# Attention before an FFN: chunks of 120 keys and paired heads, or chunks of 56 keys and four heads at a time

## The chip, the core and the metric

The kernel runs on one core of a Trainium2 chip. TensorE multiplies, VectorE (DVE) and ScalarE (ACT) do elementwise work, GpSimd (POOL) issues DMAs that convert fp32 to fp16 on the way, and SyncE (SP) and ScalarE issue DMAs that don't. The metric is the device time of one execution in microseconds; lower is better. A profiled execution has a span (first to last instruction) and a time of its own that is a little longer.

## The reference, cut to what matters

Batch 4, 8 heads, 768 positions, head size 64, 8 global keys, a local window of 96, and an FFN from 512 to 1536 and back over 3072 tokens:

```python
    scores = scale * np.matmul(q, k.transpose(0, 1, 3, 2))
    rel = pos[:, None] - pos[None, :]
    is_global = pos[None, :] < int(n_global)
    is_local = (rel >= 0) & (rel < int(n_local))
    keep = is_global | is_local
    dist = np.where(is_global & ~is_local, float(n_local), np.abs(rel).astype(np.float32))
    slopes = 2.0 ** (-8.0 * (np.arange(H, dtype=np.float32) + 1) / H)
    scores = scores - slopes[:, None, None] * dist[None, :, :]
    scores = np.where(keep, scores, -1000000000.0)
    a = np.exp(scores - np.max(scores, axis=-1, keepdims=True))
    a = a / (np.sum(a, axis=-1, keepdims=True) + 1e-09)
    attn_out = np.matmul(a, v)
    x = attn_out.transpose(0, 2, 1, 3).reshape(B * S, H * D)
    g = x @ w_gate
    silu = g * (1.0 / (1.0 + np.exp(-g)))
    out = (silu * (x @ w_val)) @ w_out
```

## The kernel before, in words

The whole program is one list of steps, the string `ORDER`. Each step is a name and its arguments (`g.0.3` is the gate product of token block 0, hidden block 3), and the loop at the end calls the function that belongs to the name. Every engine works through its own instructions in the order in which the list issues them, so the list sets the order on all engines and on the DMA queues.

**Attention.** The keys stand in 7 chunks of 120. A chunk is 128 columns of `kTs`: the 8 global keys and 120 local ones. The queries that a chunk can see are a window of 216, cut at the ends. `scores` (step `c`) puts a chunk's keys on the 128 rows of PSUM, for the two heads of a pair at once: head 0 on the upper 64 rows of TensorE, head 1 on the lower (64x128 tiles). The distances enter in one of two ways. For some units of batch 0, `bias` (step `B`) adds slope times distance by a matmul with `slopeI` before the scores; for all others `mask` (step `m`) multiplies the exponentials by `masks`, the exponential of minus slope times distance. `exps` (step `x`) is the exponential on ScalarE, to fp16 tiles `at`. `weigh` (step `w`) sums `at` over the keys for four heads at a time on 128x32 tiles: what 0 with ones (the denominators, `den`), what 1 and 2 with the even and odd columns of the values (`num`). For most halves `take_num` (step `n`) copies `num` out of PSUM on ScalarE. `invert` and `spread` (steps `i`, `r`) transpose the denominators on VectorE, take reciprocals and spread them, and `scaled` (step `p`) multiplies into `xT`, the input of the FFN.

**FFN.** A token block is 384 tokens, half a batch, and there are 8. For each of 12 hidden blocks: gate product `g` and value product `v` (4 matmuls of 384 columns each), tanh on ScalarE (`t`), two operations on VectorE (`s`, `h`). The output product `o` has 36 matmuls of 512 columns per token block, in parts of three, and `e` copies and stores.

**Loads.** `ld_first` (`Lf`) loads half of the keys and queries of batch 0's first half as fp32 by SP and ScalarE, and `cast` converts them on VectorE or ScalarE. All else of q, k, v and the weights comes by GpSimd with conversion: `Lh`, `L4`, `Lr` for q and k, `Lv` for v, `Lw` and `Lo` for the weights. Batch 0 and half of batch 1 are transposed by TensorE (`T`, `U`) and copied out (`k`, `q`, `kw`, `qw`); the other half of batch 1 and batches 2 and 3 by DMA transposes on SP (`D`), after which `K` spreads the keys into chunks on VectorE. `fill` issues matmuls on ones, which compute nothing that is used.

**PSUM.** Two double tiles take the scores and `num`, four single ones all else. They are handed out in the order in which they come free.

Of the kernel before, what the change touches and what calls it, by code (L numbers as in the profile page):

```python
# [14 lines left out]
FAR = 60000.0  # L15
KC = 120
WIN = 216
BANK = 432


def _build_dist(S, NG, NL):


    row = np.arange(128)[:, None]
# [8 lines left out]
    d = np.concatenate([first, inner, inner[:, :168], inner[:, :48]], axis=1)  # L33
# [16 lines left out]
T.3.1.0 Lw.0.2.0 k.3.1.V T.3.1.1 g.0.6 w.0.0.1.0 c.0.2.2 Lw.0.2.1 Lw.1.1.1 t.0.6 i.0.0.1 s.0.6  # L50
r.0.0.1 Lw.1.2.0 c.0.2.3 g.0.7 Lr.1.1.7 q.3.1.A x.0.2.2 v.0.2 h.0.2 w.0.0.1.1 t.0.7 s.0.7 w.0.0.1.2
# [73 lines left out]
def kernel(  # L125
# [110 lines left out]
    def release(key):  # L236
        freed.append(busy.pop(key))
# [442 lines left out]
```

## Time and profile before

| | us |
|---|---|
| runs | 253.18, 252.24, 250.27; median 252.24 |
| the profiled execution | 250.97 |
| its span | 249.2 |

| engine | busy us | share of the span |
|---|---|---|
| TensorE matmul (PE) | 237.3 | 95% |
| VectorE (DVE) | 174.0 | 70% |
| ScalarE (ACT) | 119.4 | 48% |
| GpSimd (POOL) | 77.7 | 31% |

In the profile's lines, `L530` is line 530 of the kernel; `num<-at,vS` names what is written and read; `128*32` behind a matmul is its tile of TensorE (rows x columns), and `128x216` its moving operand. A group's row gives its count, its busy time and the mean ns of one, then the time that its engine stood idle just before such instructions and what ended it. A line of the chain that ended last gives start, length and what ran. Timelines put instructions of a kind together and show in brackets how long the engine had been idle and what released it. Matmuls overlap, so a busy TensorE is not one at its peak rate.

### The profile page before, as it was taken

Reading aid. Unit: us, or ns where it says so; the run is one execution under the profiler, and the core shown is the slowest. Engines: PE = TensorE matmul, PEld = TensorE weight load, DVE = VectorE, ACT = ScalarE, POOL = GpSimd, SP = SyncE. Lnnn points to the kernel's source line nnn. Section 1 sums busy time; section 2 is a strip of 40 time slices with the busy share of each in tenths; the row PEclk is TensorE's granted clock in tenths of the full one; section 3 lists DMA queues with packets and bytes.
Section 4 is the critical chain, followed back from the end, with each engine's and each line's share of the span. In section 5 each row is a group of like instructions: output and inputs, shape, how many; then the busy total and the mean of one; then the engine's idle time right before and its main releaser. Section 6 shows DMA issues by size and latency. Waiting matters only on the chain.

```text
span 249.2 us, 5795 instructions
## 1 busy us (share of the span) xinstructions
PE 237.3 (95%) x2368; PEld 134.1 (54%) x2368; DVE 174.0 (70%) x407; ACT 119.4 (48%) x216; POOL 77.7 (31%) x99
## 2 busy tenths in 40 slices
PE   7999999997899999999999999999999899899993
PEld 4565656654455545555555565565555654455552
DVE  6598899838878696848796588789675748566210
ACT  3677773863666423575264454456464233223310
POOL 8995665762898564650000000000000000000000
PEclk9999999999999999999999999999999999999999
DMA  8999999999999999999202214120110111010202
GB/s 182 166 198 190 205 198 195 175 134 151 202 157 121 138 131 153 171 168 104 74 3 74 86 35 116 25 76 0 45 42 0 45 45 42 1 42 3 84 21 107
DMA packets 88715, 25.56 MB, mean 103 GB/s; under 512 B 78536, under 2 KB 85744, under 8 KB 88688
## 3 DMA queue, kind: packets, MB, share of 16 engines
q0 software_dynamic: 67520, 13.81, 70.2%
q1 hardware_dynamic: 20480, 10.86, 21.4%
q10 hardware_dynamic: 688, 0.52, 0.7%
q8 instruction: 18, 0.29, 0.5%
q14 instruction: 9, 0.07, 0.1%
HBM read 28.58 MB, written 6.29 MB: 140 GB/s over the span
## 4 chain that ended last, share of the span: by engine, by line
PE 77%; DMA 11%; DVE 9%; issue 1%; ACT 1%; SPq 0%; DVEq 0%; ACTq 0%
PE vps L576 22%; PE ops L610 21%; PE gps L576 21%; DMA kN<-kst 7%; PE sc L471 4%; DMA qT<-qst 3%; PE num L530 3%; DVE xT L562 2%; PE den L530 2%; PE sc L458 2%; DVE at L498 2%; DVE hT L592 2%; PE trs L361 1%; DMA k<-in_k_dram 1%; PE ops L607 1%
## 5 line engine op out<-in xcount | busy, mean ns | idle before, releaser
L576 PE MATMUL gps<-xT,wg 128*128 128x384 f16 x384 | 73.9, 326 | 2.2 <-DVE xT L562 1.6
L582 ACT ACTIVATE th<-gps 128x384 f32<-128x384 f32 x96 | 46.5, 492 | 57.5 <-PE gps L576 55.4
L576 PE MATMUL vps<-xT,wv 128*128 128x384 f16 x384 | 72.7, 326 | 0.0
L592 DVE TENSOR_TENSOR hT<-vps,sl 128x384 f16<-128x384 f32 x96 | 51.8, 553 | 26.0 <-PE vps L576 24.5
L586 DVE SCALAR_TENSOR_TENSOR sl<-th,gps 128x384 f32<-128x384 f32 x96 | 52.1, 548 | 20.8 <-ACT th L582 19.7
L610 PE MATMUL ops<-wo,hT 128*128 128x512 f16 x276 | 66.7, 379 | 0.0
L576 PEld LDWEIGHTS <-wg 128*128 128x128 f16 x384 | 36.2, 98 | 29.4 <-issue 4.0
L576 PEld LDWEIGHTS <-wv 128*128 128x128 f16 x384 | 36.5, 98 | 26.8 <-issue 0.9
L481 ACT ACTIVATE at<-sc 128x864 f16<-128x864 f32 (+2 forms) x52 | 41.9, 835 | 14.1 <-PE sc L471 14.1
L610 PEld LDWEIGHTS <-hT 128*128 128x128 f16 x276 | 26.3, 98 | 27.9 <-issue 0.4
L624 ACT ACTIVATE osb<-ops 128x512 f32<-128x512 f32 x23 | 13.8, 598 | 35.2 <-PE ops L610 35.1
L259 POOL DMA_DIRECT2D vS<-in_v_dram x28 | 25.1, 900 | 10.4 <-DMA kst<-in_k_dram 5.5
L498 DVE TENSOR_TENSOR at<-at,masks 128x864 f16<-128x864 f16 (+3 forms) x54 | 23.5, 477 | 0.0
L300 POOL DMA_DIRECT2D kst<-in_k_dram x20 | 16.9, 853 | 10.6 <-DMA kN<-kst 4.8
L300 POOL DMA_DIRECT2D qst<-in_q_dram x20 | 16.8, 848 | 6.1 <-DMA vS<-in_v_dram 2.8
L471 PE MATMUL sc<-qT,kT 64*128 64x216 f16 (+5 forms) x240 | 14.6, 240 | 0.9 <-DMA qT<-qst 0.9
L539 ACT COPY ns<-num 128x768 f32<-128x768 f32 x12 | 9.4, 801 | 11.6 <-PE num L530 11.6
L471 PEld LDWEIGHTS <-kT 64*128 64x128 f16 x240 | 8.2, 94 | 10.2 <-issue 6.4
L562 DVE TENSOR_TENSOR xT<-ns,rb 128x384 f16<-128x384 f32 x24 | 12.8, 546 | 0.5
L530 PE MATMUL num<-at,vS 128*32 128x216 f16 (+6 forms) x576 | 12.5, 226 | 0.5 <-ACT at L481 0.2
L530 PEld LDWEIGHTS <-vS 128*32 128x32 f16 x576 | 10.1, 96 | 4.1 <-issue 3.8
L545 DVE STREAM_TRANSPOSE dT<-den 128x384 f32<-128x384 f32 x16 | 9.3, 578 | 3.2 <-PE den L530 3.1
(58 smaller groups left out, 121.1 us busy)
## 6 DMA issues: line engine op xcount, KB each, us to landing
out_dram<-osb SPq DMA_DIRECT2D x23, 256.0 KB, 2.2
vS<-in_v_dram POOLq DMA_DIRECT2D x24, 120.0 KB, 8.6
qst<-in_q_dram POOLq DMA_DIRECT2D x20, 96.0 KB, 8.7
kst<-in_k_dram POOLq DMA_DIRECT2D x20, 96.0 KB, 8.8
wg<-in_moe_w_gate_dram POOLq DMA_DIRECT2D x6, 256.0 KB, 8.5
wv<-in_moe_w_val_dram POOLq DMA_DIRECT2D x6, 256.0 KB, 8.5
wo<-in_moe_w_out_dram POOLq DMA_DIRECT2D x3, 512.0 KB, 10.3
k<-in_k_dram POOLq DMA_DIRECT2D x3, 192.0 KB, 5.5
```

What stands on the lines that cost most here:

```text
L259: nc.gpsimd.dma_start(out=v_of(b)[NG:NG + n, c, :, :], in_=v[b, :, KC * c:KC * c + n, :].rearrange("h p d -> p h d"))
L300: nc.gpsimd.dma_start(out=rows_of(i, b, h // 2)[:, :, h % 2, :], in_=KQ[i][b, h].rearrange("(t p) d -> p t d", p=128))
L471: nc.tensor.matmul(sc[:, hi, col:col + n], lhsT=kTs[hp][r, 128 * c:128 * c + 128], rhs=qTs[b, hp][r, q0:q0 + n], start=fresh, stop=True, s ...
L481: nc.scalar.activation(out=at[:, :, 0:w], in_=scs.pop((b, hp, u))[:, :, 0:w], func=AF.Exp, scale=scale)
L498: ENG[e].tensor_mul(a2, a2, m[:, :, m0:m0 + n])
L530: nc.tensor.matmul(dst[r, o:o + n], lhsT=vSs[b][:, c, 4 * g + j, what - 1::2] if what else ones[:, 0:32], rhs=ats[b, hp, u][:, j % 2, col: ...
L562: ENG[e].tensor_mul(x_of(2 * b + half)[:, 2 * g + side, :], nums[b, g, half][:, side, 0:TB], rbs[b, g, half])
L576: nc.tensor.matmul(gv[t, f, which][:, 0:TB], lhsT=w[:, c, 128 * f:128 * f + 128], rhs=xTs[t][:, c, :], start=(c == 0), stop=(c == NC - 1))
L582: nc.scalar.activation(out=th, in_=gv[t, f, 0][:, 0:TB], func=AF.Tanh, scale=0.5)
L586: nc.vector.scalar_tensor_tensor(out=sl, in0=gv[t, f, "t"], scalar=1.0, in1=gv[t, f, 0][:, 0:TB], op0=AluOp.add, op1=AluOp.mult)
L592: nc.vector.tensor_mul(hTs[t][:, f, :], gv[t, f, 1][:, 0:TB], gv[t, f, "s"])
L610: nc.tensor.matmul(ops, lhsT=lhsT, rhs=wo[:, f, :], start=(f == 0), stop=(f == NFF - 1))
```

## The change

- **Chunks.** 14 chunks of 56 keys, each with the 8 global keys 64 rows; the window is 152 queries. A unit packs three windows into one PSUM bank (`UNITS`; batch 0 has its own units for each half).
- **Tiles.** `scores` works on four heads at once: two row halves of TensorE (heads of a pair) and two column halves (pairs `g` and `g + 2`), 64x64 tiles. So the 128 rows of a score tile hold two pairs of heads. `weigh` uses 64x32 tiles for `num` (row half `e`, four column tiles, two PSUM banks) and 128x32 tiles with `ones2` for the denominators of both row halves in one pass.
- **Distances.** `bias` and `slopeI` go; all units of all batches are multiplied by `masks`, which holds 4 head groups with three window forms (the second chunk has a form of its own).
- **Batch 0.** Keys and queries come as fp32 by SP and ScalarE, 16 loads of 96 rows into four buffers, and are cast. The values come as fp32 too (`Vf`, `Vt`, `VG`, `VP`), into the space that later holds `wo` and the values of batch 2, and are cast by `Vc`. `Y` writes one column of a weight tile on VectorE, so that the weight load behind it waits for that.
- **Batch 1** is transposed by TensorE alone (8 steps `U`, where there were 4 and 4 DMA transposes); `D` has 16 steps instead of 20.
- **Denominators.** `i`, `r` and `p` treat all eight heads of a half at once: 8, 8 and 16 steps instead of 16, 16 and 32. `take_num` goes: `p` reads PSUM.
- **Banks and buffers.** PSUM is one tile of eight banks, and each step names its bank (`@5`). Buffers change: `at` 14, `qT` 6, `kTs` 6, `sl` 4, `hT` ten tiles of three hidden blocks.
- **Spreading keys** (`K`) names its engine: half of the large copies go to ScalarE.
- **Order.** The list is new: 1023 steps instead of 1091. Until the first gate product it has 94 `fill` matmuls (16 before).

```diff
-KC = 120
-WIN = 216
-BANK = 432
+KC = 56
+CH = 64
+WIN = 152
+NCH = 14
...
+    near = (row < NG) & (col + KC - row < NL)
+    second = np.where(near, FAR, inner)
+    d = np.concatenate([first, second, inner], axis=1)
+    slopes = np.zeros((2, CH, 4))
+    for c in range(2):
+        for g in range(2):
+            for hi in range(2):
+                slopes[c, :, 2 * g + hi] = -(2.0 ** (-8.0 * (4 * c + 2 * g + hi + 1) / H))
+    d = np.concatenate([np.concatenate([d, d]), slopes.reshape(2 * CH, 4)], axis=1)
     return d.astype(np.float16)
 
 
 ORDER = """
...
+pre Y.0.1.0 Vf.A.5.1 Ld.S Lf.S.0.1.0 VG.S.1 Z.2 Lf.S.1.0.0 cast.0.1.0.V Z.1 Vt.S.1 Lf.S.0.2.0
+cast.1.0.0.V Li Lf.S.1.2.0 Vf.S.7.0 Vf.S.6.1 cast.0.2.0.V Z.0 VG.A.0 cast.1.2.0.V fill.26@0
+T.2.0.1@0 T.2.0.0@1 q.2.0.V Vf.S.4.0 Lf.A.0.0.0 Lf.A.0.3.1 T.0.0.1@2 Vf.S.3.0 Vt.A.0 Vf.S.1.0 M.0
+q.0.0.A cast.0.0.0.V Lf.S.0.3.0 cast.0.3.1.V fill.4@3 T.0.0.0@3 cast.0.3.0.V Lf.S.1.3.0 T.1.0.0@4
+fill.12@5 T.3.0.0@5 cast.1.3.0.V T.3.0.1@6 k.2.0.A VP.S.0.1 M.2 Vf.S.5.0 Lf.S.1.1.0 Lf.S.0.0.1
+cast.1.1.0.V k.0.0.A fill.8@7 c.0.0.0@0 Vf.S.2.0 M.3 cast.0.0.1.V T.1.0.1@7 Y.0.0.0 k.1.0.A M.1
+Vf.S.6.0 k.3.0.V Lw.0.0.0 x.0.0.0 q.1.0.V c.0.0.1@2 x.0.0.1 q.3.0.V Lf.S.1.2.1 Lf.S.0.1.1 fill.11@4
+c.0.1.1@4 x.0.1.1 T.0.1.0@0 cast.0.1.1.V c.0.1.0@1 m.0.0.0.V cast.1.2.1.V m.0.0.1.V fill.4@7
+T.2.1.1@7 T.1.1.0@3 Lw.0.0.1 Vf.S.0.0 x.0.1.0 Vf.A.0.1 m.0.1.0.V T.3.1.0@6 m.0.1.1.V fill.12@4
+w.0.0.0@4 VP.S.0.0 i.0.0 Lf.S.0.2.1 Vc.0.4.7.A Vc.0.0.4.A fill.3@5 w.0.0.1@1 w.0.0.2@4 r.0.0 p.0.0.1
+Vf.S.3.1 cast.0.2.1.A p.0.0.0 fill.10@4 T.2.1.0@4 k.3.1.A fill.4@5 g.0.0@5 k.1.1.A Lf.S.1.3.1
+k.2.1.V cast.1.3.1.A k.0.1.A T.3.1.1@1 t.0.0 Lf.S.1.0.1 cast.1.0.1.V g.0.1@2 Lf.S.1.1.1 T.0.1.1@6
+q.0.1.A cast.1.1.1.V T.1.1.1@3 Lw.0.1.0 q.2.1.A s.0.0 g.0.3@4 q.3.1.V g.0.2@0 t.0.3 VP.S.1.1 s.0.3
+c.0.0.3@6 q.1.1.V Vf.S.7.1 c.0.0.2@4 t.0.2 Lw.1.0.0 s.0.2 Lw.1.0.1 v.0.0@1 h.0.0 v.0.1@3 L4.0.4
+c.0.1.2@0 Lw.0.1.1 L4.1.0 x.0.0.3 Vf.S.1.1 t.0.1 s.0.1 x.0.0.2 m.0.0.2.V c.0.1.3@6 x.0.1.3 v.0.2@2
...
+    def windows(lo, hi, packs):
+        found = {}
+        for u, pack in enumerate(packs):
+            col = 0
+            for c in pack:
+                q0, q1 = max(KC * c, lo), min(KC * c + WIN, hi)
+                found.setdefault(u, []).append((c, col, q0, q1 - q0))
+                col += q1 - q0
+        return found
+
+    WHOLE = windows(0, S, [(0, 1, 2), (3, 4, 5), (6, 7, 8), (9, 10, 11), (12, 13)])
+    HALF0 = windows(0, TB, [(0, 1, 2), (3, 4, 5, 6)])
+    HALF1 = windows(TB, S, [(5, 6, 7, 8), (9, 10, 11), (12, 13)])
+    UNITS = {0: {**HALF0, **{u + 2: w for u, w in HALF1.items()}}}
+    for b in range(1, B):
+        UNITS[b] = WHOLE
...
+    PS = ps.tile([128, 8, 512], FP32, name="PS")
...
+    masks = sb.tile([128, 4, MW], FP16, name="masks")
...
+    NK = 6
+    kTs = [sb.tile([128, NCH * CH], FP16, name=f"kT{i}") for i in range(NK)]
+    NV = 3
+    vSs = [sb.tile([128, NCH, 4, D], FP16, name=f"vS{i}") for i in range(NV)]
...
+    def ld_first(e, i, hp, half):
+        t = h32[i, hp, half] = sb2.tile([PT, 2, JH * D], FP32, name="h32", tag="h32", bufs=4)
+        QUE[e].dma_start(out=t, in_=tokens(i, half, 2 * hp, 2 * hp + 2))
+
+    def cast(i, hp, half, e):
+        copy_on(e)(out=stage(0, i, half)[:, 2 * hp:2 * hp + 2, :], in_=h32[i, hp, half])
...
+    def wide(half):
+        t = wo.rearrange("p f d -> p (f d)")[:, 0:NCH * 4 * D] if half == 0 else vSs[2].rearrange(
+            "p i j d -> p (i j d)")
+        return t.bitcast(FP32).rearrange("p (i j d) -> p i j d", j=4, d=D)
+
+    def ld_wide(e, h, half):
+        c, j, n = h // 4, h % 4, 7 - half
+        QUE[e].dma_start(
+            out=wide(half)[CH * c + NG:CH * c + CH, 0:n, j, :],
+            in_=v[0, h, 7 * KC * half:KC * (7 * half + n), :].rearrange("(i p) d -> p i d", p=KC))
+
...
+    def put_wide_globals(e, half, c):
+        r = slice(CH * c, CH * c + NG)
+        first = wide(0)[r].rearrange("p i j d -> p i (j d)")[:, 0:1, :]
+        n = 6 + half
+        QUE[e].dma_start(
+            out=wide(half)[r].rearrange("p i j d -> p i (j d)")[:, 1 - half:, :],
+            in_=first.broadcast_to([NG, n, 4 * D]))
...
+    def cast_wide(half, i0, i1, e):
+        copy_on(e)(out=v_of(0)[:, 7 * half + i0:7 * half + i1, :, :].rearrange("p i j d -> p (i j d)"),
+                   in_=wide(half)[:, i0:i1, :, :].rearrange("p i j d -> p (i j d)"))
...
+    def gate_w(which, n, c):
+        nc.vector.memset((wg, wv)[which][:, 2 * c:2 * c + 1, WF * n:WF * n + 1], 0.0)
...
+            nc.vector.memset(ones2, 0.0)
+            nc.vector.memset(ones2[0:64, 0:16], 1.0)
+            nc.vector.memset(ones2[64:128, 16:32], 1.0)
+            nc.vector.tensor_copy(out=slope, in_=dist[:, MW:MW + 4])
...
-    def make_slope(h):
-        nc.vector.tensor_scalar_mul(slopeI[:, h, :], ident, -slopes[h] / scale)
...
+    def make_masks(x):
...
+            out=masks[:, x, :], in_=dist[:, 0:MW], func=AF.Exp, scale=slope[:, x:x + 1])
...
-    def bias(hp, u):
-        sc = scs[0, hp, u] = double("sc")
-        biased.add((0, hp, u))
-        for col, d0, n in BIAS[u // 2, u % 2]:
-            for hi in range(2):
-                nc.tensor.matmul(
-                    sc[:, hi, col:col + n],
-                    lhsT=slopeI[:, 2 * hp + hi, :], rhs=dist[:, d0:d0 + n],
...
+    def scores(bank, b, g, u):
+        at_bank["c", b, g, u] = bank
+        for c, col, q0, n in UNITS[b][u]:
             for hi in range(2):
...
+                for e in range(2):
+                    hp = 2 * e + g
+                    nc.tensor.matmul(
+                        PS[64 * e:64 * e + 64, bank + hi, col:col + n],
+                        lhsT=kT_of(b, hp)[r, CH * c:CH * c + CH],
+                        rhs=qTs[b, hp][r, q0:q0 + n], start=True, stop=True,
+                        skip_group_check=True)
...
+    def exps(b, g, u):
+        w, bank = width(b, u), at_bank["c", b, g, u]
+        at = ats[b, g, u] = sb2.tile([128, 2, 3 * WIN], FP16, name="at", tag="at", bufs=14)
         nc.scalar.activation(
-            out=at[:, :, 0:w], in_=scs.pop((b, hp, u))[:, :, 0:w], func=AF.Exp, scale=scale)
...
+    def weigh(bank, b, half, what):
+        at_bank["w", b, half, what] = bank
         parts = value_parts(b, half)
+        V = v_of(b)
...
+                if what == 0:
+                    nc.tensor.matmul(
+                        PS[r, bank, o:o + n], lhsT=ones2, rhs=at[:, hi, col:col + n],
+                        start=first, stop=last, skip_group_check=True)
+                    continue
+                for e in range(2):
+                    s = slice(64 * e, 64 * e + 64)
+                    nc.tensor.matmul(
+                        PS[r, bank + e, o:o + n], lhsT=V[s, c, j, what - 1::2],
+                        rhs=at[s, hi, col:col + n],
+                        start=first, stop=last, skip_group_check=True)
...
-    def take_num(b, g, half):
-        src = sb2.tile([128, 2, TB], FP32, name="ns", tag="ns")
-        nc.scalar.copy(out=src, in_=nums[b, g, half][:, :, 0:TB])
-        nums[b, g, half] = src
...
+    def invert(b, half):
         dT = sb2.tile([128, TB], FP32, name="dT", tag="dT", bufs=1)
-        dR = rbs[b, g, half] = sb2.tile([128, TB // 32], FP32, name="dR", tag="dR")
-        nc.vector.transpose(dT, dens[b, g, half][:, 0:TB])
-        nc.vector.reciprocal(out=dR, in_=dT.rearrange("p (n i) -> p n i", i=32)[:, :, 0])
-        release((b, g, half))
-
...
+    def spread_r(b, half):
+        dR = rbs[b, half]
+        rb = rbs[b, half] = sb2.tile([128, 2, TB], FP32, name="rb", tag="rb")
...
+    def scaled(b, half, side):
+        bank = at_bank["w", b, half, side + 1]
+        nc.vector.tensor_mul(
+            x_of(2 * b + half)[:, side::2, :], PS[:, bank:bank + 2, 0:TB], rbs[b, half])
```

## The prediction

> **What bounds the kernel now.** I read the page first, then TensorE's groups by shape, the chain that ended last, and timelines of the places where TensorE stood idle.
>
> ```profile
> span 249.2 us, 5795 instructions
> PE 237.3 (95%) x2368; PEld 134.1 (54%) x2368; DVE 174.0 (70%) x407; ACT 119.4 (48%) x216; POOL 77.7 (31%) x99
> ...
> PE   7999999997899999999999999999999899899993
> ...
> DVE  6598899838878696848796588789675748566210
> ...
> PEclk9999999999999999999999999999999999999999
> ```
>
> TensorE is busy in nearly every slice, VectorE at eight or nine tenths from 12 to 50 us. So the end is set by TensorE's work plus what it loses.
>
> ```profile
> L576 PE MATMUL gps<-xT,wg 128*128 128x384 f16 x384 | 73.9, 326 | 2.2 <-DVE xT L562 1.6 <-DVE dT L545 0.5
> L471 PE MATMUL sc<-qT,kT 64*128 64x216 f16 x144 | 11.9, 259 | 0.9 <-DMA qT<-qst 0.9
> L530 PE MATMUL num<-at,vS 128*32 128x216 f16 x192 | 9.6, 256 | 0.4 <-ACT at L481 0.2
> L458 PE MATMUL sc<-dist,slopeI 128*128 128x432 f16 x12 | 3.9, 416 | 0.1
> ```
>
> These give counts and shapes. The 326 ns is latency; the rate stands in the chain:
>
> ```profile
> 18.04 1.03 DVE xT L562 x2
> 19.11 1.30 PE gps L576 x7
> ...
> 44.44 0.79 PE trs L399 x24
> 45.23 0.76 PE gps L576 x4
> ...
> 67.65 0.65 PE ops L610 x3
> ...
> 126.11 0.48 PE sc L471 x12
> ...
> 144.23 0.61 PE den L530 x39
> ...
> 242.38 2.63 PE ops L607 x24
> ```
>
> Four 384-column matmuls take 0.65 us, three of 512 the same: about 2.4 columns per ns. The 39 `den` matmuls are quads on four column tiles; 20 of them carry 72+192+216+168+48 = 696 columns, so 39 carry 1357 and took 0.61 us (0.57 at the full rate): tiles run together. The 12 score matmuls hold 1728 columns in 0.48 us, above 2.4 per ns, so the two row halves run together as well. After another tile shape four gate matmuls take 0.76 instead of 0.65: a change of shape costs about 0.11 us.
>
> FFN: 768 x 0.1625 + 276 x 0.216 + 2.6 = 187.0 us. The last matmul ends at 242.38 + 2.63 = 245.0, so the tail is 4.2. From 19.1, where gate products run on, 225.9 us are left to it. The records after 19.1 hold FFN 186.2, scores 7.6, `num` and `den` 11.5, bias 0.9, transposes 2.2 (columns at 2.4 per ns, divided by the tiles that run together): 208.4. There are 79 changes of shape, 8.7. The remaining 8.8 are stalls; the largest:
>
> ```profile
> 59.26 0.44 PE L530 MATMUL den<-at,ones 128*32 128x216 f16 x16 [1.59 <-DVE at L498]
> ...
> 65.05 0.55 PE L471 MATMUL sc<-qT,kT 64*128 64x216 f16 x8 [0.86 <-DMA qT<-qst]
> ...
> 213.02 0.81 PE L576 MATMUL gps<-xT,wg 128*128 128x384 f16 x4 [1.58 <-DVE xT L562]
> ```
>
> The profiled run took 250.97 us, 1.8 above its span; the median of the three runs, 252.24, lies 1.3 above that.
>
> **TensorE's work after the change.** A window of 152 columns at 14 chunks, cut at the ends, is 12 x 152 + 96 + 40 = 1960 columns per head and batch; before it was 1296. In exchange, four tiles run in the scores and eight in `num`. Scores: 2 groups x 1960 x 4 batches / 2.4 = 6.5 us (41472/2 columns, 8.6, before). `den`, one pass for both row halves: 3.3; `num`, 2 x 1960 x 4 / 2.4: 6.5 (both 13.0 before). Bias 0 (7584 columns, 3.2). Transposes: 256 of 96 columns in pairs, 5.1 (144 of 128, 3.8). Together 21.4 against 28.6, FFN unchanged. Of the 7.2, 2.5 lie ahead of the first gate product (6.4 against 3.9), where TensorE waits anyway, and are worth nothing there.
>
> No row shows a 64x32 tile. Its bounds: eight together (the score row's overlap of row halves, the column quads' overlap), 6.5; row halves in turn, 13.1. I take the first, since either half of it is seen.
>
> TensorE does 94 warm matmuls instead of 16 (256 columns, 0.107 us each, 0.21 at the early half rate): 10 to 13 us, but all before the first gate product, in time that the loads and VectorE leave free.
>
> **The start, up to the first gate product.** This is where the change costs. Keys and queries of batch 0 now land as fp32 and all but a few are cast on VectorE; 16 fp32 loads stand for 4 and six that cast on the way. The present casts show the price, and the first landing:
>
> ```profile
> 4.54 0.55 DVE L344 CAST k<-k 128x384 f16<-128x384 f32 x1 [0.29 <-DMA k<-in_k_dram]
> 5.01 0.34 DVE L344 CAST q<-q 128x384 f16<-128x384 f32 x1
> ```
>
> A cast of 512 takes 0.45 to 0.73. From 4.5 us VectorE must do, before the first gate product: 12 casts (5.4 to 8.8), 3 query copies (0.55 each: 1.65), one key copy with four copies of globals (2.1), the mask products of the half (from the rows 128x432 at 377 ns and 128x864 at 599: 0.155 us + 0.514 ns per element; 2 x (0.63 + 0.93) = 3.1), 0.4 waiting on `den`, then transpose and reciprocal 0.83, the spread of 768 about 1.0, two products of 768 about 0.95 each. That ends at 20.9 with cheap casts and 24.3 with dear ones, without any gap. ScalarE's 12.0 us (four masks 2.3, key and query copies 3.5, exps 3.7, one cast, two casts of values 1.8) fit beside it. SP issues at 0.35 to 0.49 us each; a value load on which `Vc` waits is its 25th, so about 11.5 us plus 3 to land, later if an fp32 load ahead of it waits for one of four buffers: then the value loads and `VP` queue behind it. I take 22.3 for the first gate product, 3.2 later than 19.1. Weights on POOL are held by the `Y` memsets, until about 13 us; with the 8.5 us that a weight load took to land behind a full queue, the first gate weights are there at 22, and earlier with POOL's queue empty of batch 0.
>
> **After it.** Work: FFN 187.0, 3 + 8 transposing steps 3.0, scores 5.8, `num` and `den` 8.7: 204.5. Changes of shape in the new order: 73, 8.0 us. Stalls: 8.8 now. The 0.86 goes, as batch 1 no longer uses DMA transposes. The 1.59 goes: six products of 864 stood in a row there, and a batch's products shrink to 5.9 us. The 1.58 goes: the `xT` products wait no longer for a ScalarE copy of `num`, and VectorE's transposes, spreads and products per batch fall from 9.9 us (4 x 0.58, 4 x 0.23, 4 x 0.57, 8 x 0.55) to 7.5. What comes late next is VectorE right behind the start. From the first gate product to the first scores of batch 1 it has 21.6 us (16 FFN operations 8.8, masks 4.0, copies and casts 5.1, the chain of the second half 3.7), ScalarE 21.2, TensorE 16.9 + 19 changes x 0.11 = 19.0. That is a new 2.6. Stalls: 8.8 - 0.9 - 1.6 - 1.6 + 2.6 = 7.3; bounds 2 (all planned away) and 12 (none goes, the shortage doubles).
>
> Keeping `num` in PSUM until `p` holds five of eight banks for some 4 us; the FFN then turns on three, and this is in the upper bound. Moving key spreads to ScalarE and batch 0's loads off POOL costs nothing, with ScalarE at 48% and POOL empty after 125 us.
>
> Sum: 22.3 + 204.5 + 8.0 + 7.3 + 4.2 = 246.3, with 1.8 around it **248.1**. The same execution before was 250.97; a median could lie up to 1.3 higher. I give 248.3.
>
> **A rule against it.** The row first: 39 `den` matmuls in 0.61 us, 15.6 ns from start to start. The Trainium skill, TensorEngine Tiling (Array Packing), section Instruction Overhead, says that each matmul carries about 60 cycles and that tiling a dimension that is already small gains nothing. By that rule, at 2.4 per ns, an estimate of 25 ns each, the new 1744 attention matmuls would take 43.6 us instead of 16.3, and the sum would be 275. The trace disagrees (39 would take 0.98 us), so I give it 0.01.
>
> **Rivals.**
> *Issue limits the eight tiles (slower), 0.12.* `num` after asks for eight pairs of weight load and matmul per 152 columns, one per 7.9 ns; the trace shows no long stretch denser than 15.6. If that is the floor, 1024 matmuls take 16.0 instead of 6.5, +9.5: 257.8. It decides from about 12.7 ns. Against it: in the `den` row the pieces of 48 and 72 columns, at such a floor 62 ns per quad instead of 20 and 30, would make 0.73 of 0.61.
> *The start stretches (slower), 0.16.* Casts at the dear end, four fp32 buffers holding up SP: first gate product at 25.5 and the shortage behind it 5: +5.6, 253.7, on the edge.
> *The new order covers nearly everything (faster), 0.29.* Eight freely assigned banks, VectorE with less work in batches 1 to 3: gate products at 21.5, stalls 2: 240.2 + 1.8 = 242.0. For it: from 125 us on, TensorE stands idle for only 0.0 to 1.6 us in 25 even now.
> *Row halves run in turn, the tiles don't do what they say, 0.02:* +6.6, 254.9.
>
> **Numbers.** Forecast 0.40. Within 1% of 252.24 (249.7 to 254.8) is what a measurement here can't tell from no change. Of the forecast 0.26 lies below 249.7, 0.09 within, 0.05 above; the covered start and order add 0.29 below; the stretched start 0.07 within and 0.09 above; the rest 0.15 above. Faster 0.55, same 0.16, slower 0.29. The forecast's own range is 244 to 253; to hold eight in ten it must reach the covered case and most of the issue case: 240 to 258.
>
> **What would show it.** First gate product at 22 us, `num` at 0.38 us per first half and side (912 columns), `den` the same; slices of VectorE at nine tenths from 12 to 45 us; changes of shape still 0.11. Wrong if `num` takes 0.87 or more (56 matmuls at 15.6 ns), if gate products start after 25, or if stalls behind 60 us exceed 5.

## The result, and the profile after

The changed kernel takes 264.8 us (median of four runs, 264.62 to 266.58), the kernel before 252.59 beside it (four runs, 250.27 to 253.18): ratio 1.0517, interval 1.0436 to 1.0598. It is slower, and outside the forecast's range of 240 to 258. The profiled execution took 264.83 us, 13.9 more than the one before.

From the page of the changed kernel:

```profile
span 262.9 us, 7398 instructions
...
PE 243.0 (92%) x3162; PEld 142.6 (54%) x3162; DVE 162.4 (62%) x361; ACT 108.4 (41%) x204; POOL 68.2 (26%) x91
...
PE   7696499499999999999999999999999699999994
...
DVE  2357258646683485688298768966586567813840
...
PEclk9689779979999999999999999999999999999998
...
q8 instruction: 24, 0.39, 0.6%
...
L582 PE MATMUL PS<-xT,wg 128*128 128x384 f16 x384 | 72.9, 330 | 0.0
...
L367 PE MATMUL PS<-ones 128*128 128x256 f16 x94 | 17.2, 349 | 2.3 <-DVE ones L343 1.2
...
L540 PE MATMUL PS<-at,vS 64*32 64x152 f16 (+4 forms) x1024 | 10.7, 220 | 6.8 <-issue 6.8
```

TensorE's slices have holes at 4, 4 and 6 tenths (26 to 33, 46 to 53, 204 to 210 us) that the kernel before did not have. Its clock was less than full in the first 60 us, where before it read 9 throughout. VectorE, which I had expected at nine tenths from 12 to 45 us, has eight at most before 125 us and nine in two slices behind it. The group `L540` (`num`) shows the new kind of wait: 6.8 us of idle time that ended with "issue", that is, with no semaphore and no data.

The chain that ended last, at the start and at the other two holes (start, length, what ran):

```profile
14.14 5.91 DMA h<-in_k_dram
20.05 0.02 issue
20.07 0.42 DVE st L252
20.50 0.54 DVE at L507
21.04 0.35 DVE st L252
21.39 0.04 issue
21.43 0.70 PE PS L387 x24
22.13 1.42 PE PS L367 x12
23.55 0.51 PE PS L534 x28
24.06 0.43 PE PS L367 x3
24.50 0.91 PE PS L540 x86
25.41 3.16 issue
28.57 0.41 PE PS L540 x12
28.98 0.02 issue
29.00 0.97 DVE xT L569
29.98 0.04 issue
30.02 2.29 PE PS L367 x10
32.31 0.46 PE PS L387 x5
32.77 0.97 PE PS L367 x4
33.73 1.28 PE PS L582 x4
...
49.00 3.61 issue
...
208.26 2.62 issue
```

Read from the top: a load of keys ends at 20.05, and the cast that waited for it (`L252`, data of the second half of batch 0) stands ahead of the mask products `L507` on VectorE. Then 24 transposes of the second half and 12 fills (`L367`) stand ahead of `den`. In `num` TensorE stops for 3.16 us. After that 14 fills, at half clock, stand ahead of the first gate product, which comes at 33.5 to 33.7 (17.6 before, 22.3 in the forecast; a group of the chain begins a little after its first matmul).

Where the 13.9 us are: counting each matmul's columns at 2.4 per ns, divided by the tiles that run together and without fills, the kernel before had done 54.6 us of TensorE's work by 75 us, the changed one 34.2. It is 20.4 behind there, with 7.1 less to do in all (205.8 against 212.9; 7.2 in the forecast). From 75 us to the last matmul (245.0 and 259.1) it takes 14.1 us longer for 13.3 us more of work. So all but 0.8 us is lost before 75 us; behind that the 2.62 us at 208 eat what the rest of the new order gains.

**The wait with no semaphore.** The page's `q8 instruction` row is the queue that brings instructions: 24 blocks in 0.39 MB, 16 KB each (18 blocks before). I counted TensorE's instructions in the trace (weight loads, matmuls and a few others) up to each hole, and noted when the nearest block was under way:

```
hole begins   instructions started   block starts, lands   TensorE resumes
 25.41         705 =  2 x 256 + 193     26.34    27.30          28.57
 49.00        1473 =  5 x 256 + 193     50.09    50.98          52.60
208.26        5569 = 21 x 256 + 193    207.95   209.34         210.88
```

At all three holes the count stands at 193 behind a multiple of 256, and TensorE goes on 1.3 to 1.6 us after a block lands. In the kernel before the count stood at most 118 behind such a multiple when the block in question landed. That gave the theory for the experiments, **supply**: instructions come in blocks of 256, a block is asked for some 290 instructions ahead (the trace shows no request; the earliest blocks began at a count 100 short of a multiple, 293 ahead of such an end), and a burst that runs through these before it lands stops. The rival, **tiles**: 64x32 tiles get in each other's way, so that a hole belongs to certain matmuls. The third hole speaks against it even here, for it stands ahead of a `den` matmul (`L534`), in a 128x32 tile:

```profile
206.49 1.76 PE L540 MATMUL PS<-at,vS 64*32 64x152 f16 x184
210.88 0.65 PE L534 MATMUL PS<-at,ones 128*32 128x48 f16 x36 [2.62 <-issue]
```

### The profile page after: what moved, and what is told of

The parts are those of the page before. It is cut to its first block, busy times and chain, and to the rows that moved or that the text cites. A ratio compares the mean times of both kernels' runs of the same rounds, so it can differ in the third digit from the quotient of the medians.

```text
span 262.9 us, 7398 instructions
## 1 busy us (share of the span) xinstructions
PE 243.0 (92%) x3162; PEld 142.6 (54%) x3162; DVE 162.4 (62%) x361; ACT 108.4 (41%) x204; POOL 68.2 (26%) x91
## 3 DMA queue, kind: packets, MB, share of 16 engines
q1 hardware_dynamic: 25894, 14.10, 21.5%
## 4 chain that ended last, share of the span: by engine, by line
PE 84%; DMA 7%; issue 4%; DVE 2%; ACT 1%; SPq 0%; DVEq 0%
PE PS L582 47%; PE PS L617 23%; DMA h<-in_k_dram 5%; PE PS L540 4%; PE PS L477 3%; PE PS L367 2%; DMA h<-in_q_dram 2%; PE PS L534 2%; PE PS L428 1%; PE PS L614 1%; DVE at L507 1%; PE PS L387 1%; ACT at L486 1%; DVE st L252 0%; DVE xT L569 0%
## 5 line engine op out<-in xcount | busy, mean ns | idle before, releaser
L588 ACT ACTIVATE th<-PS 128x384 f32<-128x384 f32 x96 | 44.5, 491 | 78.4 <-PE PS L582 69.8
L582 PE MATMUL PS<-xT,wg 128*128 128x384 f16 x384 | 72.9, 330 | 0.0
L582 PE MATMUL PS<-xT,wv 128*128 128x384 f16 x384 | 72.7, 326 | 0.0
L592 DVE SCALAR_TENSOR_TENSOR sl<-th,PS 128x384 f32<-128x384 f32 x96 | 50.2, 547 | 32.7 <-ACT th L588 32.5
L599 DVE TENSOR_TENSOR hT<-PS,sl 128x384 f16<-128x384 f32 x96 | 51.2, 553 | 23.5 <-PE PS L582 21.4
L617 PE MATMUL PS<-wo,hT 128*128 128x512 f16 x276 | 65.1, 379 | 0.0
L486 ACT ACTIVATE at<-PS 128x912 f16<-128x912 f32 (+1 forms) x40 | 31.5, 826 | 15.6 <-PE PS L477 10.6
L507 DVE TENSOR_TENSOR at<-at,masks 128x912 f16<-128x912 f16 (+5 forms) x56 | 22.6, 441 | 5.1 <-ACT at L486 5.0
L569 DVE TENSOR_TENSOR xT<-PS,rb 128x768 f16<-128x768 f32 x16 | 14.9, 952 | 8.3 <-PE PS L540 7.9
L367 PE MATMUL PS<-ones 128*128 128x256 f16 x94 | 17.2, 349 | 2.3 <-DVE ones L343 1.2
L540 PE MATMUL PS<-at,vS 64*32 64x152 f16 (+4 forms) x1024 | 10.7, 220 | 6.8 <-issue 6.8
L367 PEld LDWEIGHTS <-ones 128*128 128x128 f16 x94 | 10.7, 122 | 6.1 <-DVE ones L343 1.2
L540 PEld LDWEIGHTS <-vS 64*32 64x32 f16 x1024 | 9.3, 91 | 8.4 <-issue 7.8
```

What stands on the lines that cost most here:

```text
L367: nc.tensor.matmul(PS[:, bank, 0:256], lhsT=ones[:, 0:128], rhs=ones[:, 0:256], start=True, stop=True)
L486: nc.scalar.activation(out=at[:, :, 0:w], in_=PS[:, bank:bank + 2, 0:w], func=AF.Exp, scale=scale)
L507: ENG[e].tensor_mul(a2, a2, m2)
L540: nc.tensor.matmul(PS[r, bank + e, o:o + n], lhsT=V[s, c, j, what - 1::2], rhs=at[s, hi, col:col + n], start=first, stop=last, skip_group_ ...
L582: nc.tensor.matmul(PS[:, bank, 0:TB], lhsT=w[:, c, 128 * f:128 * f + 128], rhs=xTs[t][:, c, :], start=(c == 0), stop=(c == NC - 1))
L588: nc.scalar.activation(out=th, in_=PS[:, gv[t, f, 0], 0:TB], func=AF.Tanh, scale=0.5)
```

## The experiments

Each run stood beside one of the kernel before, at 251.0 to 251.8 us. The same code reaches the first gate product up to 1.4 us earlier or later from one execution to the next (e1 and the changed kernel have the same start), so single times are read to some 1.5 us, and I compare the times of single products of the FFN ("product 60": its matmuls, counted from the first gate product). Kernels with the function `tiny` have their lines six further down (`L546` is `num`, `L588` the gate and value products).

**e1, three output parts moved into batch 3's weigh steps.**

```diff
-r.3.0 o.5.2.1 o.5.2.2 o.5.2.3 m.3.1.4.V Lv.3.5.0.13 Lv.3.2.0.13 w.3.0.2@2 w.3.0.1@0 m.3.0.4.V
-e.5.1 p.3.0.1 p.3.0.0 w.3.1.2@4 e.5.2
+r.3.0 m.3.1.4.V Lv.3.5.0.13 Lv.3.2.0.13 w.3.0.2@2 o.5.2.1 w.3.0.1@0 o.5.2.2 m.3.0.4.V
+e.5.1 p.3.0.1 p.3.0.0 w.3.1.2@4 o.5.2.3 e.5.2
```

> Edit: in the changed kernel's list the output parts o.5.2.1, o.5.2.2 and o.5.2.3 move from ahead of w.3.0.2 to behind w.3.0.2, w.3.0.1 and behind w.3.1.2, so that fewer of TensorE's small instructions of batch 3 stand in a row. The work is the same. Supply theory (TensorE's instructions arrive in blocks of 256, 16 KB each, and a dense burst runs to the end of what has landed): the stall at 208 us falls from 2.62 to 0.7 to 1.3 us, and what is left of it still stands 193 instructions behind a multiple of 256; the time falls by 1.3 to 2 us. Tile theory (64x32 tiles conflict in the weigh burst): the stall stays at 2.6 us, at the same matmul of w.3.0.

Measured 261.91 (span 259.2, 3.7 less). The hole at 208 is gone altogether; across it the run gains 2.1 us, the other 1.7 were there before 60 us. The holes at 25 (2.35) and 48 us (3.27) stay, again at 705 and 1473. The tiles theory, which kept the hole, fails here.

**e2, without the last 14 fills.**

```diff
-p.0.0.0 fill.10@4 T.2.1.0@4 k.3.1.A fill.4@5 g.0.0@5
+p.0.0.0 T.2.1.0@4 k.3.1.A g.0.0@5
```

> Edit: the changed kernel without fill.10 and fill.4 just ahead of the gate product g.0.0 (14 matmuls on ones that compute nothing used). If these fills hold the first gate product: it comes at 30.9 instead of 33.5 us, and the time falls by about 2.6. If something else (weights, xT) is late as well, it stays at 33. Supply theory: the stall at 25.4 stays as it is (the fills stand behind it); the one at 49.0 stays 193 instructions behind a multiple of 256, that is 28 instructions later in the code than before. Tile theory: the stall at 49 stays at the same matmul.

Measured 263.76. The first gate product comes at 29.8, 3.7 earlier. Of that, 0.3 is there before the hole, 0.8 is a shorter hole (2.36), and from the hole's end to the gate product it takes 2.3 us instead of 4.9: the fills cost 2.6. The hole near 49 us came again at count 1473, now 14 matmuls later in the code (45 left of that step behind it, where 59 were left before). Supply named that place; tiles did not.

**e3, the start in another order.**

```diff
-cast.0.1.1.V c.0.1.0@1 m.0.0.0.V cast.1.2.1.V m.0.0.1.V fill.4@7 T.2.1.1@7 T.1.1.0@3
+c.0.1.0@1 m.0.0.0.V m.0.0.1.V
...
-m.0.1.0.V T.3.1.0@6 m.0.1.1.V fill.12@4 w.0.0.0@4
+m.0.1.0.V m.0.1.1.V cast.0.1.1.V cast.1.2.1.V w.0.0.0@4
...
-fill.3@5 w.0.0.1@1 w.0.0.2@4 r.0.0
+w.0.0.1@1 w.0.0.2@4 T.2.1.1@7 T.1.1.0@3 T.3.1.0@6 r.0.0
```

> Edit: in the changed kernel the two casts of the second half (cast.0.1.1, cast.1.2.1) go behind the mask products of the first half on VectorE; the transposes T.2.1.1, T.1.1.0, T.3.1.0 of the second half go behind the weigh steps of the first; and the fills from fill.4@7 to fill.4@5 (33 matmuls) go. Some 114 instructions fewer stand ahead of the first weigh burst on TensorE. Supply theory: the boundary at which the stall of 3.16 us stood now falls behind the burst, where TensorE waits for VectorE anyway: the stall goes, and the first gate product comes at 26 to 28 instead of 33.5; the time falls by 5.5 to 7.5. Tile theory: a stall of some 3 us stays in w.0.0.1 or w.0.0.2, and the first gate product comes at 29 to 31. Third theory, that the loads set the start: the first gate product stays behind 32.

Measured 265.7, first gate product at 29.6: a miss. The hole did not go. It moved, from the timeline (start, length, what; in brackets the idle time ahead):

```profile
29.27 0.40 PE L387 MATMUL PS<-ident,st 96*64 96x96 f16 x10 [2.98 <-issue]
```

It stands in the transposes now, no longer in the weigh steps, and at count 705 once more. The request had moved back with the rest (the count that precedes the other landings by some 290 was passed at 22.8 us), and the block landed at 28.03. Of the 3.9 us that the first gate product gained, 3.4 were gone by product 60 of the FFN.

**e4, the kernel before with 150 short matmuls ahead of a weigh step.** No 64x32 tile is in it.

```diff
+    def tiny(n):
+        tag = freed[0]
+        dst = named("tiny", tag)
+        for i in range(n):
+            r = slice(32 * (i % 4), 32 * (i % 4) + 32)
+            nc.tensor.matmul(dst[r, 0:8], lhsT=ones[:, 0:32], rhs=ones[:, 0:8],
+                             start=True, stop=True, skip_group_check=True)
...
-w.2.0.1.1 w.2.0.1.2
+tiny.150 w.2.0.1.1 w.2.0.1.2
```

> Edit: the kernel before with 150 matmuls of 8 columns on ones, in 128x32 tiles as the denominators use, into a free PSUM bank just ahead of w.2.0.1.1 (near 143 us). They compute nothing that is used. No 64x32 tile is in it. Supply theory: the 300 instructions take some 2 us and the weigh steps behind them run into the end of the landed blocks: a stall of 0.5 to 2.5 us without a semaphore, with TensorE's count of instructions 193 behind a multiple of 256, beside the landing of a block; together 2.5 to 4.5 us longer there. Tile theory (only 64x32 tiles stall): the 150 matmuls cost 1.5 to 2.4 us and no idle time that no semaphore ends.

Measured 257.65 against 251.2. Timeline:

```profile
144.95 1.36 PE L348 MATMUL tiny<-ones 128*32 128x8 f16 x150
146.16 0.38 PE L538 MATMUL num<-at,vS 128*32 128x72 f16 x10
148.53 0.87 PE L538 MATMUL num<-at,vS 128*32 128x216 f16 x28 [2.00 <-issue]
```

The hole is there, in the old kernel with its old tiles, at count 3265 = 12 x 256 + 193; the block landed at 147.17. Between products 500 and 600 the run falls 5.1 us behind: 1.21 for the 150 matmuls, 2.0 the hole, and 3.41 us at half clock behind it, some 1.7. That is above the 2.5 to 4.5 expected, because the clock was not in it. (Of the other 1.4 us of the run, 1.2 are there by product 200, behind a longer wait for VectorE at 57 us: 2.81 instead of 1.59.) Tiles as a cause of the holes is out.

**e5, e3 with 200 instructions more.** In TensorE's idle time near 7 us, 100 matmuls of 8 columns.

```diff
-fill.26@0
+fill.26@0 tiny.100@0
```

> Edit: the start order of e3 and, behind fill.26 in TensorE's idle time near 8 us, 100 matmuls of 8 columns on ones more, in 128x32 tiles, which compute nothing used: 200 instructions MORE than e3. Supply theory: the block that arrived too late in e3 is now asked for some 6 us earlier, near 16 us instead of 22.8, while TensorE waits for the loads; the stall of 2.98 us at 29 goes, or stands under 0.8 us in the weigh burst; the first gate product comes at 26.5 to 28 instead of 29.6. Any theory by which more work or denser work at the start stalls TensorE (tiles, power): the stall of 3 us stays and the first gate product comes at 29.5 or later.

Measured 264.66. The hole in the start is gone (the count that was passed at 22.8 us in e3 is passed at 15.2), and the first gate product comes at 27.3:

```profile
22.18 0.95 PE L540 MATMUL PS<-at,ones 128*32 128x152 f16 x26 [1.24 <-DVE at L513]
23.18 1.80 PE L546 MATMUL PS<-at,vS 64*32 64x152 f16 x112
24.92 1.04 PE L393 MATMUL PS<-ident,st 96*64 96x96 f16 x24
...
52.28 2.05 PE L434 MATMUL PS<-ident,st 96*64 96x96 f16 x46 [4.25 <-issue]
```

More instructions, earlier, take a hole away: a supply that runs ahead by count explains that, and tiles does not. But the next hole grew to 4.25 us (0.83 more at 46), and by product 60 only 0.5 of the 6.2 us was left.

**e6, products and transposes spread over the second half's weigh steps (with e1).**

```diff
-w.0.1.0@2 Vf.S.2.1 U.1.1@3 Lo.0 Vf.S.4.1 Vc.1.4.7.V Vc.1.0.4.A U.0.1@5 w.0.1.2@0 U.0.0@6 i.0.1
-t.0.6 s.0.6 qw.0.A U.3.0@2 qw.1.A r.0.1 p.0.1.1 w.0.1.1@4 p.0.1.0
+w.0.1.0@2 Vf.S.2.1 Lo.0 Vf.S.4.1 Vc.1.4.7.V Vc.1.0.4.A t.0.4 s.0.4 v.0.4@3 i.0.1 w.0.1.2@0 t.0.6
+s.0.6 v.0.6@7 r.0.1 h.0.4 g.0.7@6 p.0.1.1 h.0.6 v.0.5@3 t.0.7 s.0.7 h.0.5 w.0.1.1@4 U.1.1@0
+qw.1.A U.1.0@1 kw.1.A p.0.1.0
```

> Edit: e1 and, in the second half of batch 0, the value products v.0.4, v.0.6, v.0.5 and the gate product g.0.7 go between the three weigh steps w.0.1.0, w.0.1.2 and w.0.1.1, and the batch 1 transposes U.1.1, U.0.1, U.0.0, U.3.0, which stood between them, go behind, among the gate products of the next token block. The work is the same. Supply theory: between the request and the end of the landed block lie some 2.7 us more of work, so the stall of 3.27 us (3.61 in the changed kernel) near 50 us falls to under 1.5, and with it some of the half clock that followed; the time falls by 2 to 4.5 against e1 (261.9). Tile theory: the stall stays over 3 us. If the second half's loads or VectorE set the end there, the stall goes and the time falls by under 1.

Measured 264.94: the hole shrank as supply said, the time did not.

```profile
51.27 0.30 PE L540 MATMUL PS<-at,vS 64*32 64x96 f16 x11 [0.95 <-issue]
...
55.17 1.44 PE L582 MATMUL PS<-xT,wg 128*128 128x384 f16 x4 [1.55 <-DVE xT L569]
```

My order put the key copies of batch 1 ahead of `p.0.1.0` on VectorE, so the next block's products waited for `xT`.

**e8, six buffers for the fp32 loads.**

```diff
-tag="h32", bufs=4
+tag="h32", bufs=6
```

> Edit: the changed kernel with six instead of four buffers for the fp32 loads of keys and queries (and ones, and the fills, 240 instead of 256 columns wide, for the room). Buffer theory: SyncE's loads waited for casts to free a buffer; the first mask product, at 20.42, comes 1 to 3 us earlier, and the first gate product with it. Bandwidth theory (the 16 DMA engines are busy throughout from 8 to 24 us at about 215 GB/s): the loads land no earlier in sum, the first mask product stays within 0.7 us of 20.4. In both the stalls of the instruction supply stay (3 to 3.6 us).

Measured 265.78. The first mask product comes at 21.5, 1.1 later than in the changed kernel and outside both ranges expected, though within the scatter of a start; the first gate product comes at 33.9. More buffers brought nothing forward, so they were not what held the start. That the loads share what the DMA engines move fits this, but this run does not show it.

**e9, the second half's loads, casts and transposes behind the first half's (with e1 and e5).**

```diff
-x.0.0.1 q.3.0.V Lf.S.1.2.1 Lf.S.0.1.1 fill.11@4 c.0.1.1@4
+x.0.0.1 q.3.0.V Vf.S.0.0 VP.S.0.0 Lf.S.0.3.1 Lf.S.0.0.1 Lf.S.1.2.1 Lf.S.0.1.1 Vf.S.5.1 Vf.S.6.1
+c.0.1.1@4
...
+p.0.0.0 g.0.0@5 cast.0.3.1.V T.3.1.0@6 cast.0.0.1.V T.0.1.0@0 k.3.1.A Lf.S.0.2.1 Vt.S.1 Vt.S.0
```

> Edit: e1 and e5 together, and at the start nothing of batch 0's second half ahead of what the first half needs: its loads (Lf.0.3.1, Lf.0.0.1, Lf.1.2.1, Lf.0.1.1, Vf.5.1, Vf.6.1, Vf.0.1, Vt; 0.98 MB ahead of the last value load of the first half) go behind the first half's on the queues, its casts and transposes behind the first gate product; fill.11 goes. Load theory (the DMA engines move some 200 GB/s throughout, so 0.98 MB are 4.8 us of the start): the first gate product comes at 22 to 24 instead of 27.3 (33.5 in the changed kernel), and the last load of the first half lands 4 to 5 us earlier. Rival, VectorE's and ScalarE's chain sets the start: it stays behind 26. For the total: if the second half's loads set what follows, as the four variants that came together again near 58 us let me think, the time falls to 259 to 262 only; if the start is worth its full size, to 255 to 258.

Measured 275.8. The first gate product comes at 24.3, 3.0 earlier than in e5: 0.98 MB of other loads ahead of it were worth at most that (casts, transposes and 11 fills went from ahead of it too), less than the 4.8 us reckoned. The total went the other way: I had put the casts behind `p.0.0.0`, SyncE stood without a free buffer from 15.7 to 24.6, and TensorE waited for the rest:

```profile
24.32 1.44 PE L588 MATMUL PS<-xT,wg 128*128 128x384 f16 x4 [2.18 <-DVE xT L575]
...
31.47 0.53 PE L393 MATMUL PS<-ident,st 96*64 96x96 f16 x8 [4.29 <-ACT st L252]
...
38.58 0.53 PE L393 MATMUL PS<-ident,st 96*64 96x96 f16 x8 [5.18 <-ACT st L252]
...
61.80 1.05 PE L434 MATMUL PS<-ident,st 96*64 96x96 f16 x35 [3.80 <-issue]
```

Two more things made it slow: the granted clock was half from 18.1 to 45.4 us, and supply stopped TensorE three times more, for 1.17 us at 55, 3.80 at 58 and 2.20 at 128, each at count 193 behind a multiple of 256.

**e10, e11, e12: can the first 60 us be mended by order?** e11 is e6 with `p.0.1.0` ahead of the key copies; e10 adds e5's start with `g.0.1`, `g.0.3`, `g.0.2` ahead of the waiting transposes; e12 is e10 with batch 1's loads behind the weights.

```diff
-h.0.5 w.0.1.1@4 U.1.1@0 qw.1.A U.1.0@1 kw.1.A p.0.1.0
+h.0.5 w.0.1.1@4 U.1.1@0 p.0.1.0 qw.1.A Lw.1.2.0 U.1.0@1 g.1.4@5 kw.1.A
...
-g.0.0@5 k.1.1.A Lf.S.1.3.1 k.2.1.V cast.1.3.1.A k.0.1.A T.3.1.1@1 t.0.0 Lf.S.1.0.1 cast.1.0.1.V g.0.1@2
+g.0.0@5 k.1.1.A Lf.S.1.3.1 k.2.1.V g.0.1@2 k.0.1.A t.0.0 cast.1.3.1.A s.0.0 g.0.3@4 T.3.1.1@1
...
-Lw.1.1.0 m.0.1.4.V Lw.1.1.1 x.0.0.4
+Lw.1.1.0 m.0.1.4.V Lw.1.1.1 L4.1.0 L4.0.0 L4.0.4 L4.1.4 x.0.0.4
```

> Edit: e1, the start of e5 with the gate products g.0.1, g.0.3 and g.0.2 ahead of the second half's transposes that wait for its loads, and e6's spreading of the second half's weigh steps, with the product p.0.1.0 on VectorE now ahead of batch 1's key copies (in e6 it stood behind kw.1.A, and the products of the next block waited 1.55 us for it). Supply theory: no stall without a semaphore over 1.5 us is left in the run; the time falls to 254 to 260. If spreading only moves the wait (as in e6, where 3.3 us came back by 62 us): 261 to 265, with the loss between 30 and 62 us.

> Edit: e6 with the product p.0.1.0 ahead of batch 1's key copies on VectorE, and the transposes of batch 1 one by one between gate products; the start is that of the changed kernel. If the wait for p.0.1.0 was what gave e6's gain back: 258 to 260.5 (e1 261.9, e6 264.9), with the products behind 62 us 2 to 4 us ahead of e1's. If VectorE and ScalarE are short there in any order: 262 to 265.

> Edit: e10 with batch 1's four loads of keys and queries (L4, 1.5 MB) behind the gate and value weights (Lw.0.1.1, Lw.1.1.0, Lw.1.1.1) in GpSimd's queue instead of ahead of them, and the transpose U.2.0 of batch 1 behind the others. Load-order theory (in the first 60 us the DMA engines move 200 GB/s without a pause, and what TensorE waits for is what stands behind other bytes): the two waits for wv in e10 (1.04 and 0.81 us near 44) go and products 80 and 150 of the FFN come 2 to 4 us earlier than in e10 (60.6 and 73.5); the time falls to 258 to 260.5. If the rest (half clock, ScalarE's and VectorE's chains) sets it: the waits go and the time stays at 261 to 263. If batch 1's loads then come too late: its transposes wait, over 263.

Measured 262.1, 265.92 and 264.77: in none did the time fall as the supply theory alone would have it. In e10 no hole of over 0.6 us ended with "issue" is left, yet product 80 of the FFN comes at 60.6 (62.4 in the changed kernel, 60.8 in e1). Other waits have come in:

```profile
43.95 0.50 PE L588 MATMUL PS<-xT,wv 128*128 128x384 f16 x2 [1.04 <-DMA wv<-in_moe_w_val_dram]
45.25 0.50 PE L588 MATMUL PS<-xT,wv 128*128 128x384 f16 x2 [0.81 <-DMA wv<-in_moe_w_val_dram]
...
58.98 0.39 PE L483 MATMUL PS<-qT,kT 64*64 64x152 f16 x12 [1.61 <-ACT qT L447]
```

In e12 the weights come in time, and the casts of values come late instead (2.01 us at 44.9), then the key copies (1.22 and 1.08 near 58). In e11 the wait for `p.0.1.0` fell from 1.55 to 0.30 us, and a new hole of 2.18 us opened from 57.5 to 59.7, in the transposes, at a count of 193 again.

**e13, half of `num` left out; e14, e1 and e2 together, timed.**

```diff
-                for e in range(2):
+                for e in range(1):
```

> Edit: the changed kernel with only the upper row half in num (w steps 1 and 2 with e = 0 alone): 512 matmuls and their 512 weight loads left out, half of the sums for xT are not computed. Supply theory: a weigh half is now 168 or 216 instructions instead of 280 or 360, less than lies between the request and the end of a landed block (293); the stalls at 25.4 and 208 us go, the one at 49 (where 256 instructions of transposes stand in between) falls under 2.5; num takes 5 us less (512 x 9.6 ns). The time falls by 8 to 13, to 252 to 257, if the freed time in the first 60 us is not taken by other waits; by 5 to 8 if it is. Theory that num costs only its columns (6.4 ns each, no part in the stalls): the stalls stay and the time falls by 3 to 4.

> Edit: e1 and e2 together, the two edits that shortened the run by themselves (by 2.9 and 1.1 against the changed kernel). If their gains add up: 260.5 to 261.5, ratio to the kernel before 1.035 to 1.045. If the start's 2.6 us are absorbed before 60 us, as in e3 and e5: 261.5 to 262.5. In no case below 258.

e13 computes only half of the sums for `xT`, so it shows a cause and is no version to use. It took 255.16, its profiled span is 252.2: 10.7 less than the changed kernel's, within what supply allowed, and no hole with "issue" of over 0.6 us is left. By 75 us it is 7.1 ahead, where two holes had cost 6.8; across the hole at 208 it gained 3.1. From 75 to 186 us, where the changed kernel has no hole, it gained only 0.5; so the gain is near the size of the three holes (9.4), not that of 512 matmuls at 9.6 ns. The timelines show why. The same last step of batch 3, of the changed kernel:

```profile
211.46 0.73 PE L540 MATMUL PS<-at,vS 64*32 64x48 f16 x72
212.12 1.47 PE L582 MATMUL PS<-xT,wg 128*128 128x384 f16 x8
```

and of e13:

```profile
200.82 0.64 PE L540 MATMUL PS<-at,vS 64*32 64x48 f16 x36
201.40 1.48 PE L582 MATMUL PS<-xT,wg 128*128 128x384 f16 x8
```

From start to next start, 72 matmuls on eight tiles take 0.66 us, 36 on four take 0.58. The row halves do run together, and the starts of the single matmuls in the trace tell where this ends. On eight tiles the first 30 of a step start at the pace of their columns (this step: within 169 ns, where columns at 2.4 per ns on eight tiles ask for 174). Behind some 35, at full clock, each follows the one before by 8.3 to 8.7 ns, where its columns ask for 5.0 to 6.8. On four tiles they keep to the pace of their columns (30 in 418 ns, 400 by the columns). So half of the matmuls take nearly as long as all, and 9.6 ns each is not what leaving one out saves.

e14 took 261.63 (four runs, 261.06 to 263.34), ratio to the kernel before 1.0363, interval 1.0316 to 1.041. It is as fast as any whole version here and still slower. The median is 3.2 below the changed kernel's, where the gains of e1 and e2 together are 3.9. It lies 0.1 above the range expected if they add up, and its four runs scatter by 2.3, so whether they do stays open. The profiled one is the slowest of the four (263.34), and its hole near 50 us is 4.38 long. No whole version beats the kernel before.

## Why the prediction was wrong

**TensorE's work: right in total.** The records of the two kernels differ by 7.1 us; the forecast had 7.2.

**`num` at 6.5 us, eight tiles together: right for the start of each step, too little for the rest.** Away from holes a half with 112 matmuls takes 1.06 us, one with 144 takes 1.3, together 9.4. The forecast of 0.38 us per first half and side measured 0.53; my bound of 0.87 for "wrong" was not reached. Some 0.9 of the 9.4 is the change of shape behind each of the eight halves (0.11 each), which the sum has apart. The other 2.0 above 6.5 fit the pace of 8.3 to 8.7 ns behind the first matmuls of a step (e13). The 150 matmuls of e4, 8 columns each, give what I had no row for: their first 32 come in rounds of four, one on each column tile, 25 ns from most rounds to the next; behind the 35th each follows after 8.3 ns; together 1.21 us. So *Issue limits the eight tiles* named a limit that is there, but at 15.6 ns put it nearly twice too high; it lies under the 12.7 from which that rival decides, and costs some 2 us, not 9.5. *Row halves run in turn* fails.

By the rule of the Trainium skill, TensorEngine Tiling (Array Packing), section Instruction Overhead, 60 cycles would be, an estimate at 2.4 per ns, 25 ns each. Read for one tile's own matmuls, the rounds of e4 agree with it; read for all matmuls in a row, as my prediction did, e4 disagrees by a factor of three.

**The step that failed: the first gate product at 22.3 us.** It came at 33.5. The 11.2 us come apart like this:
- 3.2, the hole in `num` (present in e3, gone in e5). I priced instructions by the time that each takes and never asked whether they arrive. The counts were at hand: the forecast has "one per 7.9 ns; the trace shows no long stretch denser than 15.6" in it, and used that for a rate alone.
- 2.6, fills (e2), which I had costed at nothing "in time that the loads and VectorE leave free". The last 14 stood behind the products on which the gate product waits, and ran at half clock.
- 3.0, loads of the second half ahead of the first's (e5 against e9). I had summed VectorE's work and SyncE's issues; bytes were in no term.
- 2.4 is left: 24.3 in e9 against 22.3, and 0.4 that no run assigns.

e5 and e9 also changed the order of casts and transposes, and e9 has 11 fills less than e5; the split between the last three terms holds to the 1.4 us by which a start varies.

**"Stalls: 7.3", new order.** Between 53 and 208 us TensorE has no gap of over 0.3 us left, better than the 7.3 assumed; but the two holes at 49 and 208 us, 6.2 together, came in their place. No term of the sum had the half clock either, from the gate product at 33.5 to 35.8 and from 52.9 to 56.3 (5.7 us, worth some 2.9). From the first gate product to the end of the span it takes 229.4; the forecast had 224.0, or 216.7 without its stalls. With 6.2 of holes, 2.9 for the clock and 1.8 for `num` behind the gate product that makes 227.6; the last 1.8 I can't place. The shortage of VectorE (2.6) did not come in this run.

**The rivals.** *The start stretches* named the place, not the causes: 25.5 was its worst, without a word on instructions. That a wait could come for which no semaphore stands in the code was in no rival, and the range was therefore too narrow above.

**What is not settled.** The hole's cause is shown: it moves with the count (e2, e3), goes with a spread (e1), goes with more instructions ahead (e5), comes in the old kernel (e4) and goes with fewer (e13). All 33 stops of over 0.5 us that end with "issue" in these traces stand at count 193, ahead of matmuls in 64x32, 128x32, 96x64 and 128x128 tiles alike. What holds the first 60 us once the holes are gone (e10, e12) isn't one thing that these runs name: loads, casts, weights and half clock take turns there, while the DMA engines move some 200 GB/s for most of that time. No experiment here shows why a count of 193, and not 256, ends the supply, nor what sets the pace of 8.3 ns.

## What to carry to other kernels

Count TensorE's instructions per microsecond, weight loads too: a stretch of some 290 without a break stopped here when it ran in 2.8 us or less late in the run (between 2.9 and 3.7 for less than half a microsecond or not at all), and in 5.6 us or less under the loads of the first 60 us (of a dozen between 6.2 and 7.4, one stopped for longer than that). Three or four large matmuls between the pieces, or a request made earlier, shortened such a stop or removed it. Smaller tiles save columns and cost instructions, so look at both. In a start that the loads set, order the bytes by who needs them first, and keep warming matmuls out of the path behind the last wait.

## What the runs showed of the hardware that was not expected

Blocks of 256 instructions stopped TensorE for 0.5 to 4.4 us, each time at 193 behind a multiple of 256, and it went on 1.2 to 1.6 us after the block had landed. From a count of 100 short of the multiple of 256, most blocks landed 1 to 3 us later in the quiet part of the run and 4 to 10 us later under the loads before 60 us.

Short matmuls, each with its own weight load, start at the pace of their columns on all eight tiles for the first 30 of a row (229 ns for 30 in the first halves, 238 by the columns), and 8.3 to 8.7 ns apart behind some 35. On one tile the pace of very short ones is 25 ns (e4, rounds of four).

The granted clock fell to half behind idle time of TensorE, in stretches of 3.41 us or two, three (10.24 in e6) or eight (27.3 in e9) times that. Two windows of the changed kernel (the number ahead of the DMA share is the granted clock):

```profile
28.99:35.82 6.83, 5.80 (x36) 3.25 (x36) 3.42 (x8) 0.49 (x1) 0.71 (x1) 0.50 1.23 203
...
52.88:56.30 3.42, 3.42 (x101) 2.74 (x78) 1.41 (x3) 1.65 (x3) 3.42 (x6) 0.50 1.30 175
```

The Trainium skill, TensorE: Matmul & The Clock Gate, Part 1, says that the clock is set by activity in free-running windows of 3413 ns. The stretches agree with that length; the hole of 2.62 us at 208 had no half clock behind it, the one of 2.00 us in e4 had.
